# Fused attention and two mixtures of experts: when a token group's inputs are fetched, how its blocks join the next group's, and how much token work a step gets

## Chip, cores and metric

One NeuronCore of a Trainium2 chip runs the whole program in one launch. The metric is the device time of that launch in microseconds.

## The reference

Inputs are float32; q, k and v are (4, 8, 576, 64). Cut to what matters:

```python
scores = q @ k.T / sqrt(64)                      # per batch and head
kth    = 32nd largest of each row of 576
attn   = softmax(where(scores >= kth, scores, -1e9))
x  = (attn @ v) as 2304 tokens x 512
x1 = ((x @ w_a) * (x @ w_b)) @ w_out             # w_a, w_b 512 x 1536, w_out 1536 x 512
# routing: argmax and its softmax weight of normed x1 against 8 expert embeddings / tau
out[token] = gate * (relu(x1 @ w1[e]) @ w2[e])   # w1 512 x 1024, w2 1024 x 512
```

## The kernel before

Three kinds of work follow each other, and the first two overlap.

**Attention** goes tile by tile: 144 tiles of 128 query rows, in the order of `SEQ`, batch by batch, in 32 *parts* (a pair of heads with a set of rows) of 4 or 5 tiles each. The main loop counts *steps*, one a tile. For its tile, VectorE finds the 32nd largest score of each row by four MAX8 and three MATCH_REPLACE8 over 576 columns (`topk`, L380 and L383). In the same step TensorE makes the scores of the tile two steps on (`scores`, L359, evicted by ScalarE at L360) and transposes the weights of the tile four steps back (`turn`, L414, evicted at L417); ScalarE and GpSimd make these weights between (`softmax`, L392 to L397). After a part's last tile TensorE multiplies its weights with v and spreads the reciprocals of the row sums (`mix` L451, `along` L433). VectorE makes these reciprocals (`sums`, L422 adds 1e-9, L423 inverts). At the end of that step `finish` scales the result on GpSimd, splits it into a high and a low half (L463, L216, L217), and SyncE writes the halves to `xh_d` and `xl_d` (L472, L473).

**Token work** is x1 for nine *groups* of 256 tokens (`moe1`). A group's inputs are read back from `xh_d` and `xl_d` (`Group.inputs`, L595), into the tiles `raw` for odd groups and `xg` for even ones. Then come 12 *blocks*: 24 first-stage matmuls of 256 columns (L670), with weights that `Group.load` fetches a block ahead (`wab`, L607), then a product and a split on ScalarE and GpSimd (L674, L679, L626), and, two blocks later, 6 second-stage matmuls of 512 columns (L639, `second`). Each 128 tokens end in a `route` (L707, L712, L736 on TensorE) that files them under an expert.

The order on TensorE, VectorE, ScalarE and GpSimd is the order in which the program's code runs; SyncE's is made by a scheduler. `run` gives each piece of attention a share of a step's budget, and `background` writes that much token work behind it. The budget counts TensorE time in nominal us:

```python
share[0] = max((STEP0 if step < S0 else STEP) - cost, 0.0) / max(n, 1)   # L918, S0 = 38
```

`cost` is the step's own attention work. A group joins the list `todo` at the end of the step in which its last input is finished (L949 to L952), and may begin from step `w` on, that step plus `RD`; `inputs()` is called when its first block is written. When the loop ends, the rest of the token work is written alone (`while todo`).

**Experts**: after routing, eight experts' matmuls over gathered tokens.

Of the kernel before, what the change touches and what calls it, by code (L numbers as in the profile page):

```python
# [17 lines left out]
OP = mybir.AluOpType  # L18
# [11 lines left out]
AHEAD_L = 10  # L30
TL = 4
LATE = 0
STEP = 5.8
TL0 = 3
S1 = 19
F0 = 1
# [13 lines left out]
EARLY = 6  # L50
STEP0 = 4.5
D0 = 1
RD = 0
S0 = 38
RGAP = 4
DEBT = 1.0
# [26 lines left out]
def fused_kernel(  # L83
# [18 lines left out]
    pe, dve, act, pool, sp = nc.tensor, nc.vector, nc.scalar, nc.gpsimd, nc.sync  # L102
# [6 lines left out]
    NE, _, F2 = w1.shape  # L109
    NP = H // 2  # L110
    KC = DM // P
    NF = DFF // P
# [83 lines left out]
    with ExitStack() as ph:  # L196
# [70 lines left out]
        def prep(b, pr, part, n, c0):  # L267
            o = Part()
            o.b, o.pr, o.n, o.c0 = b, pr, n, c0
            o.first = now[0] + AHEAD_L  # L270
            o.lead = part == [p for bb, p in order_of_parts if bb == b][0]
            o.tail = "T" in part
            o.M = 256 if "A" in part or "B" in part else 0
            o.N = o.M + 64 * o.tail
            o.c = 2 if "B" in part else 0
            if o.lead:
                load_k(o, b, pr)
            o.qr = load_q(o)
            return o
# [107 lines left out]
        def softmax(t):  # L387
            t.w = wk.tile([P, S], F32, name="z", bufs=ZB)
            if PEN[t.n % len(PEN)]:
                dve.tensor_scalar(t.w, t.s, t.thr, HUGE, op0=OP.is_lt, op1=OP.mult)  # L390
            else:
                act.activation(t.w, t.s, AF.Relu, bias=t.bi[:, 1:2], scale=-HUGE)  # L392
            yield
            pool.tensor_scalar(t.bi[:, 0:1], t.top, -1.0, None, op0=OP.mult)
            pool.tensor_tensor(t.w, t.s, t.w, op=OP.subtract)  # L395
            yield
            act.activation(t.w, t.w, AF.Exp, bias=t.bi[:, 0:1], accum_out=t.o.sm[:, t.slot : t.slot + 1])  # L397
# [19 lines left out]
                    act.activation(th[:, sl, w], pv[:, :, src], AF.Copy)  # L417
                yield 0.107 * n5

        def sums(o):  # L420
            sl = slice(0 if o.M else 4, 5 if o.tail else 4)
            dve.tensor_scalar(o.rc[:, sl], o.sm[:, sl], 1e-9, None, op0=OP.add)  # L422
            dve.reciprocal(o.rc[:, sl], o.rc[:, sl])  # L423

        def along(o):
# [141 lines left out]
        conv = Blocks()  # L567
# [43 lines left out]
        def moe1(G):  # L611

            gi = G.gi
            g0, N = GROUPS[gi]
            G.inputs()
            xg, ws = G.xg, G.ws
            LA = WB // 2 - 1
            while len(ws) < LA:
                G.load()
            px = [None, None]  # L620
            gs = {}
            pend = []

            def tick():
                if pend:
                    pend.pop(0)[1]()  # L626

            def second(f, tiles=(0, 1)):
                while pend and pend[0][0] <= f:
                    tick()  # L630
                hi, lo = gs[f]
                if gi == 0:
                    conv.need(2, f)
                for t in tiles:
                    ts = slice(t * P, (t + 1) * P)
                    if f == 0:
                        px[t] = mp.tile([P, DM], F32, name="x1", bufs=2)
                    for i, (g, w) in enumerate(((lo, 0), (hi, 1), (hi, 0))):
                        pe.matmul(  # L639
                            px[t], g[:, ts], wo[:, w, f], start=(f == 0 and i == 0), stop=(f == NF - 1 and i == 2)  # L640
                        )
                    if f == NF - 1:
                        r = route(g0 // P + t, px[t])
                        next(r)
                        routes.append(r)
                        debt[1] = 0.0
                    tick()
                    yield 0.64

            for f in range(NF):  # L650
                nxt = todo[1][1] if len(todo) > 1 and todo[1][0] <= now[0] else None
                if f >= (NF - 4 if gi else NF - 1) and nxt:
                    nxt.inputs()
                if f + LA < NF:
                    G.load()
                elif nxt:
                    nxt.load()
                if gi == 0:
                    conv.begun = f
                    while now[0] < NRW and not (conv.ready(0, f) and conv.ready(1, f)):  # L660
                        yield None
                    for i in range(2):
                        conv.need(i, f)
                    ws[f] = [conv.tiles[i, f] for i in range(2)]
                ab = mk.tile([P, 2, GN], F32, name="gab")
                p = mp.tile([P, 2, 256], F32, name="ab", bufs=2)
                for i, wt in enumerate(ws[f]):
                    terms = [(a, x, c) for (a, x) in ((0, 1), (1, 0), (0, 0)) for c in range(KC)]
                    for j, (a, x, c) in enumerate(terms):
                        pe.matmul(p[:, i], wt[:, a, c, :], xg[x][:, c, :], start=(j == 0), stop=(j == len(terms) - 1))  # L670
                        if j % 4 == 3 and (i == 0 or j < 11):
                            tick()
                            yield 4 * N / 2400
                act.activation(ab, p, AF.Copy)  # L674
                recent[0] = ab
                yield 4 * N / 2400
                hi = mk.tile([P, GN], F32R, name="gh", bufs=LAG + 2)
                lo = mk.tile([P, GN], F32R, name="gl", bufs=LAG + 2)
                pool.tensor_tensor(ab[:, 0], ab[:, 0], ab[:, 1], op=OP.mult)  # L679
                gs[f] = hi, lo  # L680
                pend += [(f, lambda: None)] * 2
                pend.append((f, partial(act.activation, hi, ab[:, 0], AF.Copy)))
                pend.append((f, partial(pool.tensor_tensor, lo, ab[:, 0], hi.bitcast(F32), op=OP.subtract)))
                if f >= LAG:
                    yield from second(f - LAG)
            tail[0] = tail[0] if gi == len(GROUPS) - 1 else lambda: None
            for tiles in ((0,), (1,)) if gi == len(GROUPS) - 1 else ((0, 1),):
                for f in range(NF - LAG, NF):
                    for _ in range(NTF if tiles[0] >= ET else 0):
                        tail[0]()  # L690
                    yield from second(f, tiles)
# [65 lines left out]
        rows = []  # L757
# [5 lines left out]
        todo = []  # L763
        done = 0
        ready = [0]
        made = {}

        live = {}
        NRW = len(rows)
# [31 lines left out]
        now = [0]  # L801
# [41 lines left out]
        for step in range(-AHEAD_L, NRW + TL + 5):  # L843
            now[0] = step
            if step + AHEAD_L < NRW:
                b, pr, part, first, last, kind, c, slot = rows[step + AHEAD_L]
                if first:
                    with tc.high_priority(offset=FG):
                        o = made[b, pr, part] = prep(b, pr, part, len(made), c0)
# [3 lines left out]
            if 0 <= step + AHEAD_P < NRW:  # L853
                b, pr, part, first, last, kind, c, slot = rows[step + AHEAD_P]
                o = made[b, pr, part]
# [8 lines left out]
            for ahead in (1, -2):  # L864
                j = step + ahead
# [3 lines left out]
            with tc.high_priority(offset=FG):  # L869
                next(soft, None)  # L870
                soft = softmax(live[step - 2]) if 0 <= step - 2 < NRW else none
                for back in (3, 5):
                    j = step - back
                    if 0 <= j < NRW and rows[j][4] and (made[rows[j][:3]].n < F0 * NP) == (back == 3):
                        sums(made[rows[j][:3]])
                if 0 <= step < NRW:
                    cur = topk(live[step], FOLD[step % len(FOLD)])
                for _ in range(4):
                    next(thresholds[0], None)
                    next(cur, None)  # L880
                if step == NRW:
                    thresholds[0] = none
                elif 0 <= step < NRW:
                    thresholds[0] = cur
# [31 lines left out]
            if flips:  # L916
                cost, n = cost + 0.44, n + 2
            share[0] = max((STEP0 if step < S0 else STEP) - cost, 0.0) / max(n, 1)  # L918
            for slot_, g in enumerate((tg, sg, tg, mg, sg)):
# [29 lines left out]
            while done < len(GROUPS) and sum(GROUPS[done]) <= ready[0]:  # L949
                w = step + (D0 if done == 0 else RD)  # L950
                todo.append([w, Group(done, w), None])
                done += 1  # L952
        order.__exit__(None, None, None)

# [320 lines left out]
```

## Time and profile before

| | |
|---|---|
| median of 3 runs | 1390.84 us (1390.66 to 1391.62) |
| profiled execution | 1391.86 us, span 1390.1 us |
| TensorE (PE) busy | 1165.6 us, 84% of the span |
| VectorE (DVE) busy | 941.8 us, 68% |
| ScalarE (ACT) busy | 800.2 us, 58% |
| GpSimd (POOL) busy | 757.8 us, 55% |
| mean granted TensorE clock | 0.912 of full speed |

A share of the whole span averages over stages. VectorE's MAX8 of attention run from 21.4 to 952 us; the first token matmul starts at 128.5 us and the last second-stage one at 1102.9 us. Times in the rows are us from the span's start, unless marked ns. A wait is put down to what ended it.

### The profile page before, as it was taken

Reading aid. Unit: us, or ns where it says so; the run is one execution under the profiler, and the core shown is the slowest. Engines: PE = TensorE matmul, PEld = TensorE weight load, DVE = VectorE, ACT = ScalarE, POOL = GpSimd, SP = SyncE. Lnnn points to the kernel's source line nnn. Section 1 sums busy time; section 2 is a strip of 40 time slices with the busy share of each in tenths; the row PEclk is TensorE's granted clock in tenths of the full one; section 3 lists DMA queues with packets and bytes.
Section 4 is the critical chain, followed back from the end, with each engine's and each line's share of the span. In section 5 each row is a group of like instructions: output and inputs, shape, how many; then the busy total and the mean of one; then the engine's idle time right before and its main releaser. Section 6 shows DMA issues by size and latency. Waiting matters only on the chain. (4 is left out here: it accounts for less than half of the span.)

```text
span 1390.1 us, 22908 instructions
## 1 busy us (share of the span) xinstructions
PE 1165.6 (84%) x7720; PEld 997.5 (72%) x7721; DVE 941.8 (68%) x2022; ACT 800.2 (58%) x1917; POOL 757.8 (55%) x1164
## 2 busy tenths in 40 slices
PE   3566677769969977987995998699899979999996
PEld 2445555559858866876874886588788858888885
DVE  6999999968958996895888699693110125444540
ACT  4766676657747775765666677466343325444441
POOL 5765989747655774764666577366354331212200
PEclk9867878889989988998998999699999989999998
DMA  6333566437646635764663565465898326544530
GB/s 228 122 96 113 196 207 213 155 124 243 185 142 185 200 127 170 233 187 141 187 187 98 176 212 155 137 197 164 274 313 243 136 55 204 170 163 158 184 120 19
DMA packets 125708, 236.99 MB, mean 170 GB/s; under 512 B 22766, under 2 KB 71022, under 8 KB 125587
## 3 DMA queue, kind: packets, MB, share of 16 engines
q1 hardware_dynamic: 121426, 225.20, 51.2%
q0 software_dynamic: 4160, 10.29, 2.3%
q8 instruction: 62, 1.02, 0.3%
q14 instruction: 60, 0.48, 0.1%
HBM read 195.38 MB, written 40.85 MB: 170 GB/s over the span
## 5 line engine op out<-in xcount | busy, mean ns | idle before, releaser
L380 DVE MAX8 t<-y 128x8 f32<-128x576 f32 x432 | 311.3, 748 | 2.9
L395 POOL TENSOR_TENSOR z<-s,z 128x576 f32<-128x576 f32 x144 | 206.3, 1432 | 136.5 <-ACT z L392 136.2
L670 PE MATMUL ab<-xg,wab 128*128 128x256 f32 x1440 | 221.5, 298 | 42.1 <-DMA xg<-xl_d 28.4
L670 PEld LDWEIGHTS ab<-xg,wab 128*128 128x128 f32 x1440 | 196.9, 200 | 48.3 <-issue 23.0
L383 DVE MATCH_REPLACE8 y<-t,y 128x576 f32<-128x576 f32 x288 | 213.9, 743 | 0.0
L670 PE MATMUL ab<-raw,wab 128*128 128x256 f32 x1152 | 172.2, 294 | 35.7 <-DMA raw<-xl_d 28.8
L414 PE MATMUL tr<-ident,z 128*128 128x128 f32 x720 | 145.6, 305 | 62.8 <-ACT z L397 40.5
L380 DVE MAX8 t<-s 128x8 f32<-128x576 f32 x144 | 107.8, 748 | 117.9 <-ACT s L360 113.6
L670 PEld LDWEIGHTS ab<-raw,wab 128*128 128x128 f32 x1152 | 153.8, 197 | 38.5 <-issue 20.7
L360 ACT ACTIVATE s<-tr 128x288 f32<-128x288 f32 x288 | 118.9, 413 | 86.5 <-PE tr L359 84.9
L414 PEld LDWEIGHTS tr<-ident,z 128*128 128x128 f32 x720 | 96.0, 154 | 80.7 <-ACT z L397 44.4
L397 ACT ACTIVATE z<-z,bi 128x576 f32<-128x576 f32 x144 | 111.7, 775 | 69.9 <-POOL z L395 69.7
L359 PE MATMUL tr<-kT,qT 128*128 128x288 f32 x512 | 135.8, 351 | 14.2 <-ACT s L360 8.5
L639 PE MATMUL x<-wo,gh 128*128 128x512 f32 x432 | 137.9, 401 | 0.0
L417 ACT ACTIVATE wt<-tr 128x384 f32<-128x384 f32 (+2 forms) x320 | 125.5, 404 | 16.4 <-PE tr L414 16.1
L1030 POOL DMA_INDIRECT out_dram<-o,ids x24 | 23.8, 992 | 200.3 <-ACT o L1029 198.3
L1058 PE MATMUL y<-u,hT 128*128 128x512 f32 (+1 forms) x528 | 128.0, 396 | 0.4 <-DVE hT L1163 0.4
L679 POOL TENSOR_TENSOR gab<-gab 128x256 f32<-128x256 f32 x108 | 81.7, 757 | 81.0 <-ACT gab L674 68.9
L981 DVE TENSOR_TENSOR u<-raw,u 128x1024 fp32r<-128x1024 f32 x64 | 76.3, 1222 | 62.5 <-ACT u L980 62.5
L359 PEld LDWEIGHTS tr<-kT,qT 128*128 128x128 f32 x512 | 94.6, 219 | 26.0 <-ACT s L360 10.9
L392 ACT ACTIVATE z<-s,bi 128x576 f32<-128x576 f32 x144 | 111.8, 776 | 0.0
L1058 PEld LDWEIGHTS y<-u,hT 128*128 128x128 f32 (+1 forms) x528 | 89.7, 173 | 27.6 <-DVE hT L1163 0.5
(171 smaller groups left out, 2180.7 us busy)
## 6 DMA issues: line engine op xcount, KB each, us to landing
wab<-wab_d SPq DMA_DIRECT2D x192, 512.0 KB
raw<-in_moe_w_dram SPq DMA_DIRECT2D x28, 1024.0 KB
wab_d<-wab SPq DMA_DIRECT2D x24, 512.0 KB
kT_d<-kT SPq DMA_DIRECT2D x16, 576.0 KB
kT<-kT_d SPq DMA_DIRECT2D x16, 576.0 KB
vs<-in_v_dram SPq DMA_DIRECT2D x32, 256.0 KB
raw<-in_moe_w_a_dram SPq DMA_DIRECT2D x12, 512.0 KB
raw<-in_moe_w_b_dram SPq DMA_DIRECT2D x12, 512.0 KB
```

The lines of the kernel that those rows point to most:

```text
L359: pe.matmul(p, l, r, start=(i == 0), stop=(i == len(terms) - 1))
L360: act.activation(t.s[:, cs], p, AF.Copy, scale=SCALE)
L380: dve.max(v, cur)
L383: dve.match_replace(out=rest, in_to_replace=v, in_values=cur, imm_value=LOWEST)
L392: act.activation(t.w, t.s, AF.Relu, bias=t.bi[:, 1:2], scale=-HUGE)
L395: pool.tensor_tensor(t.w, t.s, t.w, op=OP.subtract)
L397: act.activation(t.w, t.w, AF.Exp, bias=t.bi[:, 0:1], accum_out=t.o.sm[:, t.slot : t.slot + 1])
L414: pe.transpose(pt[:, i * P : (i + 1) * P], t.w[:, k0 : k0 + P], ident)
L417: act.activation(th[:, sl, w], pv[:, :, src], AF.Copy)
L639: pe.matmul(px[t], g[:, ts], wo[:, w, f], start=(f == 0 and i == 0), stop=(f == NF - 1 and i == 2))
L670: pe.matmul(p[:, i], wt[:, a, c, :], xg[x][:, c, :], start=(j == 0), stop=(j == len(terms) - 1))
L1058: pe.matmul(p[:m], (hi, lo)[a], u[:, b, f % 4, :], start=(f == 0 and i == 0), stop=(f == NF2 - 1 and i == 2))
```

## The change

`STEP` goes from 5.8 to 4.8 and `RD` from 0 to 2, so from step 38 on a step gets 1.0 nominal us less token work, and a group may begin two steps after its last mix, not at once. A group's inputs are asked for in the step in which it joins the list (if at most one other group is there), with its first weights if it is alone. A group's last two blocks of second-stage matmuls, which stood alone, now each follow one block of first-stage matmuls of the next group, if that group's first weights have been asked for. The addition in `sums` goes from VectorE to GpSimd, and from the reciprocal's step to the one before (for the first four parts to the same step).

```diff
-STEP = 5.8
+STEP = 4.8
...
-RD = 0
+RD = 2
...
-        def sums(o):
+        def sums(o, add):
             sl = slice(0 if o.M else 4, 5 if o.tail else 4)
-            dve.tensor_scalar(o.rc[:, sl], o.sm[:, sl], 1e-9, None, op0=OP.add)
+            if add:
+                pool.tensor_scalar(o.rc[:, sl], o.sm[:, sl], 1e-9, None, op0=OP.add)
+                return
             dve.reciprocal(o.rc[:, sl], o.rc[:, sl])
...
             tail[0] = tail[0] if gi == len(GROUPS) - 1 else lambda: None
+            nxt = todo[1] if len(todo) > 1 and todo[1][0] <= now[0] and todo[1][1].ws else None
+            if nxt:
+                nxt[2] = moe1(nxt[1])
             for tiles in ((0,), (1,)) if gi == len(GROUPS) - 1 else ((0, 1),):
                 for f in range(NF - LAG, NF):
+                    for _ in range(6 if nxt else 0):
+                        yield next(nxt[2])
                     for _ in range(NTF if tiles[0] >= ET else 0):
                         tail[0]()
                     yield from second(f, tiles)
...
                     if 0 <= j < NRW and rows[j][4] and (made[rows[j][:3]].n < F0 * NP) == (back == 3):
-                        sums(made[rows[j][:3]])
+                        if back == 3:
+                            sums(made[rows[j][:3]], True)
+                        sums(made[rows[j][:3]], False)
+                j = step - 4
+                if 0 <= j < NRW and rows[j][4] and made[rows[j][:3]].n >= F0 * NP:
+                    sums(made[rows[j][:3]], True)
...
                 todo.append([w, Group(done, w), None])
+                if done and len(todo) < 3 and conv.ready(1, NF - 1):
+                    todo[-1][1].inputs()
+                    if len(todo) == 1:
+                        todo[-1][1].load()
```

The number of TensorE instructions is the same. Counted in the two orders, up to the transposes of the last attention tile there stood 1992 first-stage and 480 second-stage matmuls and 12 of the 18 routings, and now 1680, 405 and 10; behind it 600, 168 and 6, and now 912, 243 and 8.

First place: TensorE, where group 2 begins (L451 and L433 are the mix that finishes its inputs; the `x_` tiles are the results of group 1; `xg_` are the inputs of group 2). Before:

```order
L639 MATMUL x_3430<-wo,gl 128x512
L639 MATMUL x_3430<-wo,gh 128x512 x2
L359 MATMUL tr<-kT,qT 128x288 x2
L414 MATMUL tr<-ident,z 128x128 x2
L451 MATMUL tr<-wt,vs 64x256 x10
L433 MATMUL tr<-ident,rc 64x128 x4
L359 MATMUL tr<-kT,qT 128x288 x2
L414 MATMUL tr<-ident,z 128x128 x3
L670 MATMUL ab<-xg_4605,wab 128x256 x4
L670 MATMUL ab<-xg_4603,wab 128x256 x8
```

And now:

```order
L414 MATMUL tr<-ident,z 128x128 x3
L672 MATMUL ab<-xg_4403,wab 128x256 x4
L359 MATMUL tr<-kT,qT 128x288 x2
L672 MATMUL ab<-xg_4401,wab 128x256 x8
L414 MATMUL tr<-ident,z 128x128 x2
L672 MATMUL ab<-xg_4403,wab 128x256 x4
L359 MATMUL tr<-kT,qT 128x288 x2
L672 MATMUL ab<-xg_4401,wab 128x256 x4
L302 MATMUL tr<-identr,qs 128x128 x4
L672 MATMUL ab<-xg_4401,wab 128x256 x4
L414 MATMUL tr<-ident,z 128x128 x3
L641 MATMUL x_3570<-wo,gl 128x512
```

Group 1 was finished before that mix, and two rows behind the mix group 2 began. Now the mix stands 62 rows above the first row of group 2, and group 2's first block comes before group 1's last second-stage blocks.

Second place: SyncE, where group 2's inputs are read (L472 and L473 write the last halves, L595 reads). Before:

```order
L472 DMA xh_d<-xh 128x256
L473 DMA xl_d<-xR 128x256
L595 DMA xg_4603<-xh_d 128x4x256
L595 DMA xg_4605<-xl_d 128x4x256
L607 DMA wab<-wab_d 128x1024 x6
L296 DMA kT<-kT_d 128x1152
```

And now:

```order
L474 DMA xh_d<-xh 128x256
L475 DMA xl_d<-xR 128x256
L597 DMA xg_4401<-xh_d 128x4x256
L597 DMA xg_4403<-xl_d 128x4x256
L609 DMA wab<-wab_d 128x1024 x4
L296 DMA kT<-kT_d 128x1152
```

On SyncE nothing moved at this place: the reads still stand right behind the last write. Fewer weight loads follow before the next keys.

## Rows read from the trace of the kernel before

**Rows 1.** Busy time by stage; the first line names the columns.

```profile
core 0: us, PE busy (x) PEld busy (x) DVE busy (x) ACT busy (x) POOL busy (x), PEclk, DMA share, GB/s
273.10:951.30 678.20, 583.66 (x4268) 503.39 (x4267) 556.63 (x1273) 449.51 (x1171) 421.00 (x711) 0.92 0.56 173
951.30:1103.10 151.80, 141.26 (x974) 126.54 (x974) 16.19 (x43) 58.70 (x152) 74.06 (x150) 0.97 0.76 241
1103.10:1390.10 287.00, 268.70 (x1481) 230.14 (x1479) 115.02 (x186) 113.87 (x187) 54.16 (x70) 0.97 0.41 132
```

**Rows 2.** Waits of PE, 273.1 to 951.3: us in total, times, longest.

```profile
PE ab L670 <- DMA raw<-xl_d: 28.8, 3, 10.8
PE ab L670 <- DMA xg<-xl_d: 28.4, 3, 10.6
PE x L639 <- POOL gl L626: 11.9, 6, 4.1
```

**Rows 3.** Timeline where group 1 begins: start, duration, instruction, [idle before <- released by].

```profile
294.60 0.92 PE L433 MATMUL tr<-ident,rc 128*64 128x128 f32 x12
...
298.41 0.21 POOL L394 TENSOR_SCALAR bi<-t 128x1 f32<-128x1 f32 x1
298.47 0.32 SPq L473 DMA_DIRECT2D xl_d<-xR  x1
...
300.62 0.57 SPq L595 DMA_DIRECT2D raw<-xl_d  x1
...
305.62 1.22 PE L670 MATMUL ab<-raw,wab 128*128 128x256 f32 x4 [8.89 <-DMA raw<-xl_d]
```

**Rows 4.** DVE, groups of instructions, 273.1 to 951.3: busy, mean ns | idle before.

```profile
L380 DVE MAX8 t<-s 128x8 f32<-128x576 f32 x106 | 79.6, 751 | 117.9 <-ACT s L360 113.6 <-POOL xsb L463 3.7 <-POOL tk L155 0.3
...
L422 DVE TENSOR_SCALAR rc<-sm 128x5 f32<-128x5 f32 (+1 forms) x24 | 11.4, 475 | 0.0
...
L423 DVE RECIPROCAL rc<-rc 128x5 f32<-128x5 f32 (+1 forms) x24 | 4.4, 185 | 0.8
L722 DVE TENSOR_SCALAR st<-m,st 128x1 f32<-128x1 f32 x11 | 2.1, 195 | 0.0
...
L721 DVE MATCH_VALUE_LOAD i<-m,lg 128x8 f32 x11 | 1.0, 92 | 0.4
```

**Rows 5.** Busy time of four stretches, columns as in rows 1.

```profile
296.50:311.00 14.50, 5.61 (x33) 5.37 (x31) 5.15 (x11) 3.56 (x10) 2.67 (x5) 0.65 0.52 173
311.00:393.00 82.00, 79.09 (x616) 70.59 (x614) 73.61 (x173) 60.35 (x156) 59.15 (x97) 1.00 0.70 218
804.90:860.00 55.10, 54.92 (x416) 47.47 (x414) 53.14 (x121) 40.85 (x111) 40.02 (x70) 1.00 0.66 204
849.80:881.00 31.20, 23.16 (x143) 15.71 (x142) 30.62 (x69) 23.22 (x60) 19.34 (x41) 0.78 0.20 58
```

**Rows 6.** Timeline of PE, one block of token work behind attention.

```profile
1083.77 3.04 PE L670 MATMUL ab<-xg,wab 128*128 128x256 f32 x24
1086.64 0.40 PE L639 MATMUL x<-wo,gl 128*128 128x512 f32 x1
...
1088.03 3.04 PE L670 MATMUL ab<-xg,wab 128*128 128x256 f32 x24
```

**Rows 7.** Timeline of PE, a routing's transposes and logits, each with what follows.

```profile
1013.62 0.60 PE L707 MATMUL ab<-ident,xr 128*128 128x128 f32 x4
1013.97 2.16 PE L670 MATMUL ab<-raw,wab 128*128 128x256 f32 x16
...
1018.79 0.96 PE L712 MATMUL ab<-enT,x1T 128*128 128x8 f32 x8
1019.60 1.68 PE L670 MATMUL ab<-raw,wab 128*128 128x256 f32 x12
```

**Rows 8.** Waits of PE, 951.3 to 1103.1.

```profile
PE ab L670 <- DMA wab<-wab_d: 8.6, 3, 5.9
```

**Rows 9.** The instructions of line 422: ns min/median/max.

```profile
L422 DVE TENSOR_SCALAR rc<-sm x32: 158/241/1922, 51.1 to 962.4; 128x4 f32<-128x4 f32 x16, 128x5 f32<-128x5 f32 x16
```

## The prediction

> **What bounds the kernel now.** I read the table of busy time by stage first, because the shares over the whole span mix stages with different limits. It splits the span after the first token group into three: 273.1 to 951.3 us, where attention and token work run together; 951.3 to 1103.1 us, where only token work is left; and the experts, to the end [rows 1]. The change touches the first two. In the first the reader should see that VectorE is busy 556.6 of 678.2 us and TensorE 583.7, so neither is full: each waits for the other. In the second VectorE has almost nothing to do and TensorE is busy 141.3 of 151.8 us.
>
> Next I read who waited for whom in the first stretch. TensorE lost 57.2 us (28.8 + 28.4) in six waits for the low half of a group's inputs, one at the start of each of groups 1 to 6 [rows 2]. The timeline of one of them gives the chain: the last part's mix ends on TensorE at 295.5, GpSimd scales and splits it, SyncE writes the low half at 298.47 and starts to read it back at 300.62, and the first token matmul starts at 305.62 after 8.89 us idle [rows 3]. So data are ready about 10 us after the mix ends, and the kernel before asks for them 1.2 us after that. Because the order on TensorE is fixed, the scores behind that matmul wait too, and VectorE with them: VectorE's first MAX8 of a tile was idle 117.9 us in this stretch, 113.6 of them for scores [rows 4]. The six fetches explain half of it. The other half is steps with more TensorE work than VectorE's step: in 311 to 393 us TensorE is busy 79.1 of 82.0 us and VectorE only 73.6 [rows 5]. Between groups it is the reverse: in 849.8 to 881 us there is no token work, VectorE is busy 30.6 of 31.2 us, TensorE 23.2 [rows 5]. That uneven load is what the change evens out.
>
> **The change, part by part.** *Less token work a step.* The counts of the two orders (section on the change) say that 312 first-stage and 75 second-stage matmuls, just over one of nine groups, go from the attention stretch to behind it, with two of the eighteen routings. Their price is read where TensorE does nothing else: a block of 24 first-stage matmuls starts at 1083.77, its six second-stage ones at 1086.64, the next block at 1088.03 [rows 6]. That is 2.87/24 = 0.120 us and 1.39/6 = 0.231 us. So 312 x 0.120 + 75 x 0.231 = 37.4 + 17.3 = 54.8 us leave the first stretch and come back in the second, where nothing hides them. A routing costs TensorE 0.35 us for its transposes and 0.81 for its logits, by the starts of what follows each [rows 7], 1.2 us with its two small sums; two add 2.4 us.
>
> In the first stretch TensorE then needs at most 583.7 - 54.8 = 529 us. That still contains what six waits cost it in clock: in 296.5 to 311 us the granted clock averaged 0.65 [rows 5], which is 10.2 us at 1.2 GHz instead of 2.4, or 5.1 us of work lost. VectorE becomes the limit. Its floor: 556.6 us busy, less the additions that move off it, less the routings that move out. The 24 additions of this stretch took 11.4 us, 475 ns each [rows 4]; the eleven routings took 8.3 us in five rows, from 2.1 to 1.0 us [rows 4], 0.75 each, so two are 1.5. The floor is 556.6 - 11.4 - 1.5 = 543.7 us. ScalarE and GpSimd, busy 449.5 and 421.0 us in it [rows 1], stay below.
>
> How much VectorE will still idle is the unknown that sets the answer, and I bound it by three stretches [rows 5]. With no token work it idles 0.6 of 31.2 us, 1.9%. In 804.9 to 860, where a group thins out, 2.0 of 55.1, 3.6%, with TensorE at 54.9 of 55.1. In 311 to 393, in the thick of a group, 8.4 of 82.0, 10.2%. The new load lies below that of the second stretch, but is never absent, so I take 3.6% and keep the other two as ends: 543.7/0.964 = 564 us, against 554 and 606.
>
> *The fetch.* On SyncE the reads of a group stand behind its last writes as before (second place in the order), so the chain of 10 us is no shorter; what changes is that TensorE comes to it later. For group 1 the offset of two steps puts one more step of about 5.1 us (543.7 us over 106 steps) ahead of the first token matmul, so of 8.9 us some 3 remain, also once on VectorE. If TensorE is held by a late transpose there anyway, it is nothing. For groups 2 to 6 the previous group is still unfinished when the inputs are asked for (first place in the order: for group 2, 62 rows of TensorE's order lie between the mix and the first use, where there were two), so all of their wait goes. If a fetch were late there, the matmuls behind it and VectorE's scores would wait as now. The fetch holds SyncE's queue as it does today: the read of the low half waits for the write, and the weights, keys and queries behind it wait with it; among TensorE's thirteen kinds of wait of this stretch, of which [rows 2] has the three that matter here, none is for weights or keys, so I cost it at nothing; with that cover gone it would be one more wait of the group start's kind, 9 us.
>
> *Interleaved blocks.* They remove the waits of a group's last second-stage matmul for GpSimd's low half, 11.9 us in six [rows 2]. TensorE is no longer the limit there, so this is worth nothing further; it lies inside the 3.6%. Behind attention the next group's weights are asked for at the same rate as before, one block of 4.26 us each [rows 6]. There TensorE waited 8.6 us for weights over two groups [rows 8], so I charge 4.3 us for the third and keep 0 as the lower end.
>
> *The addition on GpSimd.* 32 small instructions more, of some 0.2 us by the small one of [rows 3]; with 421.0 us of work [rows 1] GpSimd has a quarter of 567 us free, and the addition now stands a step ahead of its reciprocal, so nobody waits. On VectorE it took between 158 and 1922 ns, median 241 [rows 9], so the gain could be as low as 24 x 0.158 = 3.8 us if the long ones only absorbed waiting that then moves to the next instruction; that lies inside the range.
>
> **Sum.** First stretch: 678.2 - (564 + 3) = 111.2 us saved. Second: 54.8 + 2.4 + 4.3 = 61.5 us added. The experts are unchanged. Net 49.7 us off the profiled 1391.86 us (its span is 1390.1; 1.8 us lie around it), so 1342.2 for that execution. It stands 1.0 us above the median of 1390.84, so I predict **1341 us**. At the ends: idle of 1.9%, no first wait and no wait for weights give 678.2 - 554 - 57.2 = 67 off, 1324; idle of 10.2% gives 678.2 - 609 - 61.5 = 8 off, 1383.
>
> **Rivals.** *Steps stay coupled (1352 to 1383).* VectorE keeps idling as in the thick of a group, 10.2%. For it: the new order still packs three full steps in a row before a mix. Against it: a step with almost no token work follows each mix and lets TensorE catch up, and in the stretch of 3.6% the load was higher.
>
> *The fetch is still waited for (up to 1395).* If all six waits stayed, 57.2 - 3 = 54 us of the saving would go: 1341 + 54 = 1395. That is the case in which the change doesn't do what it says. Against it: the order, where from group 2 on the end of the previous group stands between the fetch and its first use.
>
> *TensorE's clock (slower, 1394 to 1414).* Thinner steps leave TensorE idle after each mix, and idling is when the granted clock fell here: 0.78 in the stretch without token work, 0.65 around a wait, 1.00 in the two loaded ones [rows 5]. Price: at full clock TensorE needs 529 less six times 5.1, or 498 us. If each of the 24 parts of the stretch lost 5.1 us to one such fall, it would need 498 + 122 = 620 us, saving 58 and paying 61.5: 1394; with the coupling of 20 us on top, 1414. TensorE's spare 46 us (544 - 498) absorb the first nine falls, and the sign turns only where 498 + 5.1 n passes 678.2 - 61.5, at 23 of the 24. Against it: the stretch of 3.6% held 1.00 although its steps behind a mix were just as empty. The Trainium skill's page "TensorE: Matmul & The Clock Gate", section "Loop structure matters more than you think", speaks for this rival: it says that whether matmuls stay at the fast clock is decided by the loop nest, by dense work as against gaps. By that rule the sum would be the 1394 to 1414 of this rival; by the rows it is 1341. The trace agrees with the page about long waits, and not about the loaded steps.
>
> **Chances.** Forecast, 1324 to 1352: 0.66. Coupled steps, 1352 to 1383: 0.20. Better than 1324: 0.04. Fetch still waited for: 0.04. Clock: 0.06. The measurement can tell about 0.2%, 2.8 us. Faster than that, below 1388: 0.66 + 0.20 + 0.04 + 0.01 of the fetch case = 0.91; within it the other 0.03 of that case and 0.01 of the clock's, 0.04; slower the clock's 0.05. The range leaves out the best case, the last two and the top of the coupled one: 1322 to 1376.
>
> **What would show it.** Right: no TensorE wait for inputs in groups 2 to 8; attention's last MAX8 near 840 us instead of 952; steps of 5.2 to 5.4 us; VectorE's idle in that stretch near 20 us; token work behind attention near 210 us instead of 152; VectorE's additions gone. Wrong: VectorE idling 60 us with TensorE full (coupling), a granted clock below 0.9 in attention (clock), waits of 5 to 10 us at group starts (fetch), or blocks of more than 4.3 us behind attention (weights).

## The result and the profile after

| | before | changed |
|---|---|---|
| median | 1391.23 us (1390.66 to 1394.78, 4 runs) | **1346.26 us** (1345.10 to 1346.60, 4 runs) |
| ratio, 95% interval | | 0.9667 [0.9651, 0.9684] |
| profiled execution, span | 1391.86, 1390.1 us | 1346.58, 1344.8 us |
| mean granted TensorE clock | 0.912 | 0.939 |

The forecast was 1341 us in 1322 to 1376. Busy time by stage of the changed kernel, cut at the same places as [rows 1] but for one: attention ends here with its last MAX8, at 856.5 us (in the kernel before that is 952.0, 0.7 us behind the cut shown there).

```profile
core 0: us, PE busy (x) PEld busy (x) DVE busy (x) ACT busy (x) POOL busy (x), PEclk, DMA share, GB/s
274.40:856.50 582.10, 521.98 (x3863) 442.19 (x3862) 542.39 (x1240) 427.93 (x1125) 400.74 (x676) 0.97 0.59 176
856.50:1058.90 202.40, 196.23 (x1382) 177.56 (x1381) 17.16 (x51) 76.64 (x197) 102.84 (x210) 0.99 0.80 253
1058.90:1344.80 285.90, 268.47 (x1481) 230.19 (x1479) 115.33 (x186) 113.86 (x187) 54.16 (x70) 0.97 0.41 132
```

From step 38 to the last MAX8 attention took 678.9 us and takes 582.1: 96.8 less. Token work alone behind it took 151.3 and takes 202.4: 51.1 more. Step 38 starts 1.3 us later and the experts are 1.0 us shorter. Together that is 96.8 - 51.1 - 1.3 + 1.0 = 45.4, up to rounding the difference of the spans (45.3). VectorE is now busy 542.4 of 582.1 us, TensorE 522.0.

VectorE's waits of the changed kernel from 274.4 to 856.5 (us in total, times, longest), then the groups of its lines that answer to [rows 4]:

```profile
DVE rc L425 <- POOL rc L423: 32.7, 12, 7.9
DVE t L380 <- ACT s L360: 4.1, 4, 1.6
```

```profile
L380 DVE MAX8 t<-s 128x8 f32<-128x576 f32 x106 | 78.8, 744 | 4.1 <-ACT s L360 4.1
L425 DVE RECIPROCAL rc<-rc 128x5 f32<-128x5 f32 (+1 forms) x24 | 4.3, 179 | 32.7 <-POOL rc L423 32.7
```

The waits for scores, 113.6 us in [rows 4], are down to 4.1. In their place stands a wait that the kernel before did not have: the reciprocal waits 32.7 us for the addition on GpSimd. TensorE's waits in the same stretch, for [rows 2], and behind attention, for [rows 8]:

```profile
PE tr L414 <- ACT wt L417: 9.4, 18, 1.7
PE ab L672 <- DMA raw<-xl_d: 6.7, 1, 6.7
...
PE x L641 <- POOL gl L628: 1.6, 1, 1.6
```

```profile
PE ab L672 <- DMA wab<-wab_d: 2.9, 2, 2.0
```

Of six waits for a group's inputs (57.2 us) one is left, group 1's, of 6.7 us. The waits for GpSimd's low half fell from 11.9 to 1.6.

Where the new wait comes from is read in GpSimd's timeline, 352 to 359 us, beside VectorE's:

```profile
352.52 0.75 POOL L628 TENSOR_TENSOR gl<-gab,gh 128x256 fp32r<-128x256 f32 x1
353.24 0.21 POOL L394 TENSOR_SCALAR bi<-t 128x1 f32<-128x1 f32 x1
353.41 1.41 POOL L395 TENSOR_TENSOR z<-s,z 128x576 f32<-128x576 f32 x1
354.77 0.75 POOL L681 TENSOR_TENSOR gab<-gab 128x256 f32<-128x256 f32 x1
355.47 0.21 POOL L747 TENSOR_TENSOR rk<-rk,base 128x8 f32<-128x8 f32 x1
...
357.30 1.26 POOL L756 DMA_INDIRECT ids_d<-tk,ds  x1 [0.31 <-POOL ds L755]
358.64 0.23 POOL L423 TENSOR_SCALAR rc<-sm 128x4 f32<-128x4 f32 x1
```

```profile
351.45 0.74 DVE L380 MAX8 t<-s 128x8 f32<-128x576 f32 x1
...
355.08 0.74 DVE L383 MATCH_REPLACE8 y<-t,y 128x576 f32<-128x576 f32 x1
358.90 0.18 DVE L425 RECIPROCAL rc<-rc 128x4 f32<-128x4 f32 x1 [3.08 <-POOL rc L423]
359.00 0.73 DVE L380 MAX8 t<-y 128x8 f32<-128x576 f32 x1
359.65 0.74 DVE L380 MAX8 t<-s 128x8 f32<-128x576 f32 x1
```

The addition takes 0.23 us. It is late because GpSimd works its instructions off in their order, and a block's product, a routing's ranks and an indirect DMA stand ahead of it. VectorE also keeps its order, so the next MAX8 waits behind the reciprocal: this step, from one tile's first MAX8 to the next tile's, lasted 8.2 us where the median step lasts 5.1.

### The profile page after: what moved, and what is told of

The parts are those of the page before. It is cut to its first block, busy times and chain, and to the rows that moved or that the text cites. A ratio compares the mean times of both kernels' runs of the same rounds, so it can differ in the third digit from the quotient of the medians.

```text
span 1344.8 us, 22872 instructions
## 1 busy us (share of the span) xinstructions
PE 1158.5 (86%) x7720; PEld 987.7 (73%) x7721; DVE 925.3 (69%) x1990; ACT 796.6 (59%) x1917; POOL 768.4 (57%) x1196
## 5 line engine op out<-in xcount | busy, mean ns | idle before, releaser
L672 PE MATMUL ab<-xg,wab 128*128 128x256 f32 x1440 | 214.7, 294 | 12.7 <-POOL wab L541 8.2
L414 PE MATMUL tr<-ident,z 128*128 128x128 f32 x720 | 142.5, 300 | 73.3 <-ACT z L397 44.9
L672 PEld LDWEIGHTS ab<-xg,wab 128*128 128x128 f32 x1440 | 192.1, 196 | 17.7 <-POOL wab L541 9.0
L672 PE MATMUL ab<-raw,wab 128*128 128x256 f32 x1152 | 175.0, 295 | 14.4 <-DMA raw<-xl_d 6.7
L359 PE MATMUL tr<-kT,qT 128*128 128x288 f32 x512 | 133.3, 346 | 14.6 <-ACT s L360 9.3
L453 PE MATMUL tr<-wt,vs 128*64 128x256 f32 (+3 forms) x640 | 101.9, 458 | 12.7 <-ACT s L360 10.7
L628 POOL TENSOR_TENSOR gl<-gab,gh 128x256 fp32r<-128x256 f32 x108 | 81.7, 757 | 53.1 <-ACT gh L628 47.9
```

Source lines behind the costliest of these rows:

```text
L359: pe.matmul(p, l, r, start=(i == 0), stop=(i == len(terms) - 1))
L414: pe.transpose(pt[:, i * P : (i + 1) * P], t.w[:, k0 : k0 + P], ident)
```

## Experiments

Theory: the smaller step does nearly all of it, since it leaves token work over when the next group's inputs are finished; VectorE is the limit in attention; and the moved addition gives back what it saves, and more. Rivals: the early fetch does it, or the joined blocks; TensorE still sets the pace. The early fetch and `RD` 2 were run only together with other parts, never by themselves.

For all kernels, from the profiled execution: attention from step 38's first MAX8 to the last, VectorE's busy and idle time in it, and token work alone behind it.

| kernel | median us | ratio, 95% interval | attention | busy | idle | behind |
|---|---|---|---|---|---|---|
| before | 1391.23 | | 678.9 | 557.3 | 121.6 | 151.3 |
| changed | 1346.26 | 0.9667 [0.9651, 0.9684] | 582.1 | 542.4 | 39.7 | 202.4 |
| step_only | 1350.88 | 0.9709 [0.9676, 0.9742] | 578.6 | 554.7 | 23.9 | 207.4 |
| step58 | 1379.41 | 0.9911 [0.9877, 0.9946] | 669.0 | 545.6 | 123.3 | 149.5 |
| no_add | 1334.38 | 0.9586 [0.9545, 0.9627] | 568.3 | 543.3 | 25.1 | 204.3 |
| add_dve | 1340.13 | 0.9641 [0.9605, 0.9678] | 575.1 | 554.0 | 21.1 | 202.8 |
| add_early | 1336.44 | 0.9621 [0.9601, 0.9642] | 569.1 | 543.4 | 25.7 | 205.3 |
| no_join | 1348.92 | 0.9702 [0.9675, 0.9730] | 581.0 | 542.6 | 38.3 | 205.9 |
| rd3 | 1344.13 | 0.9678 [0.9653, 0.9702] | 570.3 | 543.8 | 26.4 | 209.4 |
| s44 | 1365.54 | 0.9839 [0.9804, 0.9873] | 556.1 | 541.8 | 14.3 | 245.4 |
| s50 | 1337.88 | 0.9617 [0.9599, 0.9635] | 579.1 | 544.1 | 35.0 | 195.3 |
| s52 | 1319.97 | 0.9496 [0.9469, 0.9524] | 595.2 | 545.5 | 49.7 | 167.0 |
| s55 | 1362.99 | 0.9794 [0.9771, 0.9817] | 651.9 | 546.4 | 105.6 | 150.5 |
| best | **1323.87** | 0.9527 [0.9498, 0.9555] | 593.8 | 545.4 | 48.4 | 169.5 |

### The step alone, and everything but the step

`step_only` is the kernel before with one number changed; `step58` is the changed kernel with that number put back.

```diff
-STEP = 5.8
+STEP = 4.8
```

> The kernel before with STEP 4.8 and nothing else: no earlier fetch, no offset of two steps, no joined blocks, the addition on VectorE. Theory S, that the smaller share of token work is what matters because it leaves a group unfinished when the next one's inputs are asked for: the waits for inputs of groups 2 to 6 go without the new fetch, that of group 1 stays at 9 us, and with no wait for GpSimd's addition the time lies at 1326 to 1345 us, no slower than the whole change. Theory F, that the new fetch and the joined blocks carry their own share: waits of 4 to 9 us stay at group starts and ends and the time is 1360 us or more.

```diff
-STEP = 4.8
+STEP = 5.8
```

> The changed kernel with STEP back at 5.8: new fetch, offset, joined blocks and GpSimd's addition stay. Groups then end before the next ones begin, as in the kernel before. Theory S: each group start still waits some 3 to 7 us for its inputs (the chain of 10 us less one step), steps inside a group are held by TensorE, and GpSimd's addition costs its waits: 1365 to 1395 us. Theory F: the waits at group starts are gone with the new fetch, 50 us of the 57 are saved: 1340 us or less.

The step alone gives 2.9% of the 3.3% (the two intervals overlap), the rest without it 0.9%. Its 1350.88 us is still slower than the 1326 to 1345 expected. Next to it the whole change is 3.5 us longer in attention (582.1 against 578.6), where the addition is waited for, and 5.0 shorter behind it. TensorE's first two waits of step_only in attention:

```profile
PE ab L670 <- DMA raw<-xl_d: 8.9, 1, 8.9
PE x L639 <- POOL gl L626: 8.2, 4, 2.4
```

The fetch waits of groups 2 to 6 are gone here too, without the new fetch and with `RD` 0. And in step58, with the new fetch and `RD` 2, all six stand again (VectorE's first two waits are shown with them):

```profile
PE ab L672 <- DMA xg<-xl_d: 22.4, 3, 11.3
PE ab L672 <- DMA raw<-xl_d: 19.1, 3, 6.6
```

```profile
DVE rc L425 <- POOL rc L423: 82.6, 19, 13.0
DVE t L380 <- ACT s L360: 34.7, 21, 5.1
```

So what hides the fetch is work left over from the group before, and the step size decides that; where none is left, the new fetch and `RD` 2 take off only 15.7 of 57.2 us (41.5 are left), and attention is 9.9 us shorter, less than the 11.7 us by which VectorE's busy time fell. step58 also shows how a wait travels: TensorE stalls for inputs (11.3 us, until 883.5), the token work on GpSimd stalls behind it, the addition stands behind that, and VectorE's wait (13.0 us, until 893.7) is put down to GpSimd.

### The addition

`no_add` lets the reciprocal read the row sums and drops the calls that add, so the addition of 1e-9 is left out of the computation. `add_dve` puts it back on VectorE, ahead of the reciprocal in its step. `add_early` keeps it on GpSimd, one step further ahead.

```diff
-            dve.reciprocal(o.rc[:, sl], o.rc[:, sl])
+            dve.reciprocal(o.rc[:, sl], o.sm[:, sl])
```

> The changed kernel without the addition of 1e-9 to the row sums: the reciprocal reads the sums directly, a step after the last tile's weights as now. (A row's largest weight is exp(0) = 1, so in float32 the sum plus 1e-9 is the sum.) In the changed kernel VectorE idles 38 us in attention, 30.0 of them in 11 waits of the reciprocal for GpSimd's addition. Theory 1, that this wait is the remaining loss and stands alone: attention gets 25 to 30 us shorter, 1316 to 1322 us. Rival, that TensorE or the scores are late at the same places and the wait only comes first: the idle moves to the MAX8 that waits for scores, and the time stays above 1335 us.

```diff
-                pool.tensor_scalar(o.rc[:, sl], o.sm[:, sl], 1e-9, None, op0=OP.add)
+                dve.tensor_scalar(o.rc[:, sl], o.sm[:, sl], 1e-9, None, op0=OP.add)
...
-                        if back == 3:
+                        if True:
                             sums(made[rows[j][:3]], True)
                         sums(made[rows[j][:3]], False)
-                j = step - 4
-                if 0 <= j < NRW and rows[j][4] and made[rows[j][:3]].n >= F0 * NP:
-                    sums(made[rows[j][:3]], True)
```

> The changed kernel with the addition back on VectorE, right before its reciprocal, as in the kernel before. Theory 1: the 30 us of waiting for GpSimd go, and 24 additions of 475 ns in this stretch (11.4 us, if they cost what they cost before) come back, so 15 to 20 us less than the changed kernel: 1326 to 1332 us. Rival (the wait only comes first): 1340 us or more, or, if the additions get no cheaper while GpSimd is as busy as now, the same 1346.

```diff
-                j = step - 4
+                j = step - 3
```

> The changed kernel with GpSimd's addition written one more step ahead: in the step after the next of its tile's weights, two steps ahead of its reciprocal in place of one; the order moves it up by two to nine rows on GpSimd, ahead of the token work and the splits it stood behind. Theory (the 32.7 us in which VectorE waits for the addition come from what stands ahead of it in GpSimd's queue, not from the addition itself): most of that wait goes, under 8 us are left, and the kernel comes to the one without any addition, 1333 to 1338 us. Rival (GpSimd as a whole runs a step behind, so the addition waits wherever it stands, or it now waits for the row sum of its last tile and holds GpSimd's queue): 15 us or more of waits stay or move to GpSimd's products, 1342 to 1350.

VectorE's waits in attention, first of no_add, then of add_early:

```profile
DVE t L380 <- ACT s L360: 15.2, 13, 2.1
DVE t L380 <- POOL gab L681: 6.8, 1, 6.8
```

```profile
DVE t L380 <- ACT s L360: 22.7, 17, 6.2
```

Theory 1 missed in both: no_add's 1334.38 us (1316 to 1322 expected) and add_dve's 1340.13 (1326 to 1332) lie at or next to the rivals' times. Without the addition VectorE's idle falls from 39.7 to 25.1 us, 14.6 less, and the ratio by 0.008, some 11 us (uncertain by some 6, estimated from the two intervals): of 32.7 us of waits a third to under a half were really owed to it. The rest comes back under another name, above all group 1's fetch: 7.9 us behind the addition, 6.8 behind a product in no_add, 6.2 at the scores in add_early. Written one step earlier the addition is never waited for, and the kernel comes to 1336.44 us, where 1333 to 1338 was expected; its interval lies below the changed kernel's and overlaps that of no_add. GpSimd's timeline of add_early at the place shown above:

```profile
352.03 0.23 POOL L423 TENSOR_SCALAR rc<-sm 128x4 f32<-128x4 f32 x1 [0.99 <-ACT z L397]
...
358.94 1.26 POOL L756 DMA_INDIRECT ids_d<-tk,ds  x1 [0.31 <-POOL ds L755]
```

It now stands ahead of the routing, at a price of 0.99 us of waiting for the row sum on an engine that has the time. Only its place in the order was moved, so the queue ahead of the addition was the cost, not GpSimd as an engine. Even back on VectorE, where 24 additions take 12.3 us of its busy time, the kernel comes out no slower than with the addition late on GpSimd (0.9641 against 0.9667; the intervals overlap).

### The joined blocks, and a later start

`no_join` lets a group's last two blocks stand alone again. `rd3` is no_add with one step more ahead of a group.

```diff
-            if nxt:
-                nxt[2] = moe1(nxt[1])
+            nxt = None
```

> The change with a group's last two blocks standing alone again, as in the kernel before; all else as changed. Its order has 1672 first-stage and 402 second-stage matmuls in the attention stretch, 8 and 3 fewer than the changed kernel. Theory (in the attention stretch VectorE and its waits for the addition set the pace, so joining blocks is worth nothing there; behind attention the changed kernel's tail was 202.4 us where the kernel before with only the smaller step had 207.4, and the joined blocks made that difference): attention 580 to 584 us, waits of TensorE for GpSimd's low half back, some 5 us behind attention: 1350 to 1353 us. Rival A (the joins are worth nothing anywhere, the 5 us came from the fetch): 1345 to 1348. Rival B (they kept TensorE fed within attention too): two stalls of 1.5 to 2 us at each of five group ends, 10 us in attention, and 1356 to 1362.

```diff
-RD = 2
+RD = 3
```

> The changed kernel without the addition of 1e-9 (left out of the computation: the reciprocal reads the row sums), and RD 3 in place of 2: a group may begin three steps after its last mix. Its order has 24 first-stage and 6 second-stage matmuls fewer in the attention stretch. Theory (group 1 still waits for its inputs because the 10 us from the mix's end to usable data outlast two steps; one more step of 5 us covers the rest): the wait of 6.6 us on TensorE and 6.8 us on VectorE goes, one block of 4.3 us moves behind attention: 2 to 3 us less than the same kernel with RD 2 (1334.4), 1331 to 1333. Rival (the wait is only one of several things that let VectorE idle; the time comes back as waits for scores): attention the same, 4 us more behind it, 1338 to 1340.

no_join came out 0.0035 above the changed kernel (some 5 us, the intervals overlap), of which the profiled executions show 3.5 behind attention and nothing in it, although 13.4 us of waits for the low half stand again on TensorE:

```profile
PE x L641 <- POOL gl L628: 13.4, 5, 4.5
```

Five such waits that cost attention nothing are good evidence that TensorE is no longer its limit (VectorE's waits for the addition, 29.3 us in 10 here, may cover some of them). Whether the joins are worth 0 or 5 us in all is not settled.

rd3 went against the theory. Group 1's wait fell from 6.6 to 2.4 us on TensorE, VectorE's 6.8 us behind it are gone, and attention is not shorter (570.3 against 568.3): VectorE's waits for scores rose from 15.2 in 13 to 19.8 us in 18, and 5.1 us moved behind attention. Its median is 9.7 us above no_add's, its profiled execution (1339.4) only 2.7, so the size is uncertain and the direction is not.

### How much token work a step

All without the addition, as no_add, which is the row at 4.8.

```diff
-STEP = 4.8
+STEP = 4.4
```

> The changed kernel without the addition of 1e-9 (left out of the computation), and STEP 4.4 in place of 4.8. Its order has 204 first-stage and 48 second-stage matmuls fewer in the attention stretch than at 4.8: 204 x 0.120 + 48 x 0.231 = 36 us of TensorE that come behind attention. Theory (at 4.8 VectorE is the limit of the attention stretch, with 25 us of idle left in it; a smaller step can give back only a part of that): attention 550 to 565 us where it was 568, 1352 to 1370 us, slower than 1334 by 18 to 36. Rival (TensorE still sets the pace at 4.8, so each us of token work taken away is a us of attention): both cancel, 1330 to 1338.

```diff
-STEP = 4.8
+STEP = 5.0
```

> The changed kernel without the addition of 1e-9 (left out of the computation), and STEP 5.0 in place of 4.8: 100 first-stage and 24 second-stage matmuls more in the attention stretch, 100 x 0.120 + 24 x 0.231 = 17.5 us less behind attention. Theory (the gain per us of token work pulled forward is nearly whole as long as VectorE's 543 us cover TensorE; at 5.2 attention gave back 27 of 37 us): attention 574 to 582 us, 1322 to 1328. Rival (the loss begins at once, with every step that is longer on TensorE than on VectorE): attention 585 or more, 1332 to 1336.

```diff
-STEP = 4.8
+STEP = 5.2
```

> The changed kernel without the addition of 1e-9 (left out of the computation), and STEP 5.2 in place of 4.8. Its order has 208 first-stage and 54 second-stage matmuls more in the attention stretch: 208 x 0.120 + 54 x 0.231 = 37 us come forward from behind attention. Theory (between 4.8 and 5.8 the steps pass from VectorE's length to TensorE's, and the backlog that hides the fetches runs out): TensorE needs 498 + 37 = 535 us of a VectorE floor of 543 and every uneven step costs; attention 600 to 615 us where it was 568, fetch waits on TensorE of 10 to 30 us come back, 1330 to 1350. Rival A (VectorE's 543 us still cover it, no fetch wait comes back): attention 575 to 585, 1305 to 1318, and 4.8 was too small. Rival B (already all the way at what 5.8 does): attention 650 or more, above 1365.

```diff
-STEP = 4.8
+STEP = 5.5
```

> The changed kernel without the addition of 1e-9 (left out of the computation), and STEP 5.5 in place of 4.8: 280 first-stage and 66 second-stage matmuls more in the attention stretch than at 4.8, 64 and 15 more than at 5.2, so some 11 us less behind attention than there. Theory (from 5.2 on the backlog that hides the fetches is gone and the steps are TensorE's): waits of TensorE for inputs come to 20 us or more in three groups or more, attention 615 to 640, 1328 to 1350, worse than 5.2. Rival (the backlog still holds at 5.5): one or two groups wait, attention 600 to 612, 1312 to 1325, and only the last part of the way to 5.8 loses.

At 4.4 attention gains 12.2 us and the token work costs 41.1: VectorE idles 14.3 of 556.1 us and there was little more to win; time and attention came as expected. At 5.2 it is the other way: 37.3 us leave the end, attention grows by 26.9. That is faster than the theory's 1330 to 1350, and attention's 595.2 us lies between its 600 to 615 and rival A's 575 to 585. At 5.5 the backlog is gone, and more was lost than the theory had it (1362.99 us for 1328 to 1350, attention 651.9 for 615 to 640). TensorE's waits in attention of s52, then of s55:

```profile
PE ab L672 <- DMA raw<-xl_d: 10.0, 2, 6.5
```

```profile
PE ab L672 <- DMA raw<-xl_d: 21.4, 3, 8.9
PE ab L672 <- DMA xg<-xl_d: 18.2, 3, 11.3
```

Two groups wait at 5.2, one of them for 3.5 us; at 5.5 all six wait, and the time jumps by 43 us. s50 missed: only 9.0 us left the end where 17.5 were counted, in part because TensorE waits there 8.6 us for weights:

```profile
PE ab L672 <- DMA wab<-wab_d: 8.6, 7, 2.8
```

against 3.3 in no_add. TensorE's busy time behind attention did fall, by 20.0 us (198.4 to 178.4), but its idle time rose by 11.0 (5.9 to 16.9): 5.3 of them are these waits, 1.7 a longer wait for the last tiles' weights of attention, what the other 4 are is open. Why the token work's weights are late there, and with it why 5.0 is no better than 4.8 while 5.2 is, stays open.

### A faster version

`best` is the changed kernel with STEP 5.2 and the addition of `add_early`.

> The changed kernel with STEP 5.2 and GpSimd's addition two steps ahead of its reciprocal; nothing of the computation is left out. Theory (both effects stand side by side: the early addition waits for nobody, and 5.2 fills VectorE's idle time with 37 us of token work at 27 us of attention): as the kernel without the addition at 5.2, 1318 to 1326 us. Rival (at 5.2 GpSimd and ScalarE run later behind the attention work, so the addition is waited for again): waits of VectorE for it of 10 us or more, 1330 to 1345.

1323.87 us: by the ratios 4.7% below the kernel before and 1.4 points below the changed one, with nothing of the computation left out. VectorE no longer waits for the addition; it waits 42.7 us in 23 for scores, as in s52 (42.5 in 24), which is the price of the larger step. The theory held.

## Why the prediction was right, and which step failed

The forecast of 1341 us was 5 us too low, its net gain 49.7 against 45.3 us. Both big terms were too large: attention was to save 111.2 us and saved 96.8, token work behind it was to cost 61.5 and cost 51.1. The direction and the limit were understood; that errors of 14.4 and 10.4 us nearly cancel in the sum is luck.

- **Token work moves behind attention: +61.5 forecast, 51.1 measured.** The count and the prices held: they give 54.8 + 2.4 = 57.2 us, and TensorE's busy time behind attention rose by 55.4 (140.8 to 196.2). The term for weights was mis-sized. I charged 4.3 us more for a third group; the waits of [rows 8] fell from 8.6 to 2.9 us, 5.7 less, and 57.2 - 5.7 = 51.5. Why they fell is open: step_only, with nothing but the smaller step, has 2.9 us too, s55 2.6 with less token work left and s44 8.9 with more, so a price for each group has no ground in the runs.
- **VectorE becomes the limit: right.** Floor 543.7 us forecast, 542.4 measured. Its idle time was set too low: 20 us (3.6% of 564) and group 1's 3 forecast, 39.7 measured, which makes attention 582.1 us where 567 were forecast. The 3.6% itself was fair: without the addition's wait it is 25.1 of 568.3 us (4.4%, group 1's fetch in it), with the addition back on VectorE 21.1 of 575.1 (3.7%). The median step lasts 5.1 us (5.5 before), scores are waited for 4.1 us. The coupled rival falls: its 10.2% would be 60 us.
- **The step that failed: the addition "now stands a step ahead of its reciprocal, so nobody waits".** I priced GpSimd by its share of free time. It has 31% free (busy 400.7 of 582.1 us), but it works in order, and what stands ahead of the addition (a routing with its indirect DMA, a block whose inputs are late) ran up to a step behind. VectorE waited 32.7 us; taking the wait away gives some 11 us, about what the move off VectorE saved. In hindsight, with it the forecast would have been 1341 + 11 = 1352, with the weights' 10 us less 1342, and with the 3.7 us more of group 1's wait (below) 1346.
- **Group 1 keeps 3 us of its wait: too low, it keeps 6.7.** I let two steps of offset count as one VectorE step of 5.1 us. TensorE does not wait for that step's time, only through its own work in it: it went idle at 299.00 instead of 296.73, 2.3 us later, and the data came as before (first matmul at 305.70, in [rows 3] at 305.62):

```profile
298.48 0.52 PE L414 MATMUL tr<-ident,z 128*128 128x128 f32 x3
...
300.44 0.57 SPq L597 DMA_DIRECT2D raw<-xl_d  x1
...
305.70 2.08 PE L672 MATMUL ab<-raw,wab 128*128 128x256 f32 x8 [6.70 <-DMA raw<-xl_d]
```

- **Groups 2 to 6 stop waiting: right, and for the reason given** (the group before is unfinished when the inputs are asked for). The runs add that the step size alone brings this about.
- **Joined blocks worth nothing further: right within attention**; over the whole kernel 0 to some 5 us, not settled.
- **The clock rival: refuted.** The granted clock is 0.97 in attention, where it was 0.92 [rows 1], though TensorE idles 60 us in 582. It is lowest around the one fetch wait left (columns as in [rows 1]):

```profile
293.00:309.00 16.00, 8.69 (x62) 6.74 (x57) 12.74 (x28) 7.82 (x20) 8.90 (x12) 0.76 0.54 170
309.00:392.00 83.00, 79.20 (x618) 68.67 (x618) 73.96 (x169) 64.59 (x170) 56.36 (x87) 0.99 0.63 192
403.00:440.00 37.00, 30.31 (x207) 24.98 (x207) 35.25 (x79) 25.34 (x67) 28.09 (x52) 0.92 0.49 139
```

A stretch with steps almost free of token work (403 to 440 us, TensorE busy 30.3 of 37.0) still had a mean of 0.92 (1.00 is 2.4 GHz, 0.50 the lower level of 1.2). The Trainium skill's page "TensorE: Matmul & The Clock Gate", section "Loop structure matters more than you think", says that the loop nest decides whether matmuls stay at the fast clock: dense work keeps it, a long wait for a DMA ahead of the matmuls loses it. The trace agrees on both (0.99 from 309 to 392 us, 0.76 around the wait of 6.7). A long wait is not all that cost clock here, though: the kernel before fell to 0.78 between 849.8 and 881 us [rows 5], where TensorE's longest wait was 2.7 us. The changed kernel shows nothing that low away from group 1's start; what spares it was not tested by itself.

## What to carry to other kernels

An operation moved to an engine with free time is priced by what stands ahead of it in that engine's order, not by that engine's share of busy time: look up in its timeline what it would queue behind, and write it early enough to pass that. When a transfer cannot start earlier, work left over in front of its first use hides it, and the budget that leaves it over is worth a sweep: here the best of five values lay between VectorE's floor, under which a smaller step gave little back, and an empty backlog, above which every fetch was waited for again.

## What the runs showed of the hardware

**A small VectorE operation that lasts as long as GpSimd's.** In add_dve the addition on VectorE took 0.16 to 0.17 us where GpSimd was idle (11 of 32) and up to 2.2 us where it was not ([rows 9] has the same spread). VectorE and GpSimd of add_dve, 843.2 to 846.8 us:

```profile
843.93 2.21 DVE L423 TENSOR_SCALAR rc<-sm 128x4 f32<-128x4 f32 x1
846.18 0.18 DVE L425 RECIPROCAL rc<-rc 128x4 f32<-128x4 f32 x1
```

```profile
843.33 1.12 POOL L756 DMA_INDIRECT ids_d<-tk,ds  x1 [0.29 <-POOL ds L755]
844.48 0.27 POOL L394 TENSOR_SCALAR bi<-t 128x1 f32<-128x1 f32 x1
844.68 1.43 POOL L395 TENSOR_TENSOR z<-s,z 128x576 f32<-128x576 f32 x1
846.04 0.75 POOL L681 TENSOR_TENSOR gab<-gab 128x256 f32<-128x256 f32 x1
```

It ends at 846.14, when GpSimd's product ends (846.11). All 16 of add_dve's additions that took over 0.2 us end likewise, 0.03 to 0.04 us after a GpSimd instruction. The MAX8 and the reciprocal beside it show no such spread (in add_dve the MAX8 take 720 to 764 ns, the reciprocal 177 to 193). The Trainium skill's page "SBUF — State Buffer", section "Who interferes with whom", says that a VectorE instruction in a two-port mode contends with GpSimd for a shared pair of ports, and that whoever issues first has the pair for its whole instruction while the other is blocked. The common ends fit that; that the addition runs in such a mode no run here shows. The rows add that it sat through three GpSimd instructions in a row. So the 475 ns of [rows 4] were mostly waiting (24 x 0.158 = 3.8 of 11.4 us would be work, by the shortest one of [rows 9]), and a prediction should not take such a mean for work.
